# A Fourier mixing kernel on one core: its trips through DRAM cut into parts, its first transforms reordered, its stores given to another engine

## The chip, the cores and the metric

One core of one Trainium2 chip. The metric is device time in microseconds (us). Times quoted are medians of the fast runs of a kernel. A ratio is the mean time of one kernel's fast runs over the mean time of the fast runs of the kernel before that ran in the same rounds on the same chip, so it is not quite the quotient of the two medians. A difference under 2% counts as the same.

A *product* is one matrix instruction of TensorE. A transfer *lands* when its data are in place and what waits for it may go on. The *partitions* of a tile are its rows (up to 128 here); the *free dimension* runs along a row. A transform ends where the profile models the end of its last product.

## The reference, cut to what matters

```python
def _attn_ref(x, w_r, w_i, b_r, b_i):              # x: (8, 3072, 256)
    X = np.fft.rfft(x, axis=1)
    Yr = Xr @ w_r - Xi @ w_i + b_r
    Yi = Xr @ w_i + Xi @ w_r + b_i
    # soft threshold by 0.01 on both parts
    return np.fft.irfft(Y, n=x.shape[1], axis=1)

def _moe_ref(x, mu_k, mu_r, w_k, w_v, w_r):
    x_prev = x shifted by one token
    xk = mu_k * x + (1.0 - mu_k) * x_prev;  xr = the same with mu_r
    k = np.maximum(xk @ w_k, 0.0)                  # 256 -> 1024
    return sigmoid(xr @ w_r) * (k * k @ w_v)       # 1024 -> 256
```

The 3072 points of a sequence are taken as 96 x 32. A batch (there are 8) passes through a *first* transform (96 points), a *middle* (32 points, channel mixing, threshold, 32 points back), a *last* transform (96 points back), and then the products of tokens.

## The kernel before: the parts that matter

Between first and middle, and again between middle and last, partition and free dimension change places. The kernel does that by storing a tile to DRAM and fetching it back in another order: the *bounce* of A (fetched as A2) and the bounce of V (fetched as V2). TensorE takes its products in the order in which the program issues them, and a small simulation at build time decides that order: each unit of work has a due time and needs, and the constants `READ_US` and `WRITE_US` are the simulation's estimates of a fetch and a store.

```python
def first(b, t0, t1):                  # bounce of A
    ...
    def store(k):
        nc.sync.dma_start(out=Adr[b][:, 8 * q:8 * q + 8, :], in_=a)
        ...
        if q == 3:
            at(k + WRITE_US, fetch)
    def fetch(k):                      # 4 copies, each into 32 partitions
        A2[b] = a2_pool.tile([128, NG, D], BF16, name="A2")
        for cj in range(4):
            nc.sync.dma_start(out=A2[b][32 * cj:32 * cj + 32],
                              in_=Adr[b][24 * cj:24 * cj + 24].rearrange("g n d -> n g d"))
        done["A2", b] = k + READ_US
    ...
    needs = [("x", b, q), "FT"] + [("mid", 0)] * (b == 1)

def middle(b, t0, t1):                 # bounce of V
    ...
    def fetch(k):                      # 4 copies, each into 96 partitions
        for q in range(4):
            V2[b, q] = v2_pool.tile([96, 8, D], BF16, name="V2")
        for q in (2, 3, 0, 1):
            nc.sync.dma_start(out=V2[b, q], in_=Vdr[b][:, 8 * q:8 * q + 8, :])
        done["V2", b] = k + READ_US

def v_unit(t, p):                      # the end of a tile of tokens
    ...
    for xx in range(4):
        nc.sync.dma_start(out=rows[hh, half, xx], in_=o[32 * xx:32 * xx + 32])
```

## Time and profile before

| | before |
|---|---|
| median, fast runs | 670.4 us as given; 669.4 in the rounds with the changed kernel |
| span of the profiled run | 662.8 us |
| batch 0: middle starts, last transform ends | 32.0, 84.3 us |
| TensorE's last product ends | 656.8 us |

TensorE is the bound: it is busy for 593.6 of 662.8 us. The two fetches: 384 KB go into 32 partitions of A2, or into 96 of V2, in six to seven us from issue to landing. The profile gives the size of a copy and not the partitions it goes to; those stand in the program.

### The profile page before, as it was taken

The page shows a single profiled execution, that of the slowest core. Times are in us where ns is not written, and L with a number is a line of the kernel's source. Part 1 is how long each engine was busy: PE and PEld are TensorE (multiplying, and loading weights), DVE is VectorE, ACT ScalarE, POOL GpSimd, SP SyncE. Part 2 cuts the span into 40 slices and gives each one's busy share as a digit, 9 for nine tenths or more (in the row PEclk, how much of TensorE's full clock was granted, in tenths as well). Part 3 has the DMA queues.
Part 4 walks back from the last instruction along what each step waited for, and adds up shares of the span by engine and source line. Part 5 has one row for each costly group of instructions (what it writes and reads, how often), then busy time and mean ns, then how long its engine had stood idle before and what let it go on. Part 6 is the DMA issues. An engine that isn't in the chain of part 4 may idle for free.

```text
span 662.8 us, 12033 instructions
## 1 busy us (share of the span) xinstructions
PE 593.6 (90%) x4722; PEld 435.5 (66%) x4801; DVE 483.8 (73%) x732; ACT 443.5 (67%) x469; POOL 25.2 (4%) x57
## 2 busy tenths in 40 slices
PE   4295379999999989998999989999999999999996
PEld 1273247777776767765777767766777777777764
DVE  5164368788778877797678787688677896788883
ACT  6254357767777767776577767778687767766662
POOL 5021000000000000000000000000000000000000
PEclk9689579999999999999999999999999999999999
DMA  8697996362247954488155874379233852362223
GB/s 182 119 189 166 290 213 121 79 183 65 57 112 175 230 128 111 103 227 197 33 128 128 237 146 96 88 202 207 86 104 104 223 113 68 78 183 56 65 72 88
DMA packets 75593, 90.33 MB, mean 136 GB/s; under 512 B 8976, under 2 KB 59920, under 8 KB 75536
## 3 DMA queue, kind: packets, MB, share of 16 engines
q1 hardware_dynamic: 69696, 75.53, 44.5%
q0 software_dynamic: 5840, 14.03, 12.5%
q8 instruction: 37, 0.61, 0.4%
q14 instruction: 20, 0.16, 0.1%
HBM read 53.22 MB, written 50.33 MB: 156 GB/s over the span
## 4 chain that ended last, share of the span: by engine, by line
PE 66%; DMA 17%; ACT 6%; DVE 5%; issue 3%; SPq 1%; POOL 0%; DVEq 0%; ACTq 0%; POOLq 0%
PE banks L617 22%; PE banks L575 19%; PE banks L394 11%; DMA Adr<-A 7%; DMA A<-Adr 6%; PE banks L600 4%; ACT rl L581 3%; PE banks L361 3%; PE banks L418 2%; PE banks L383 2%; ACT A L234 2%; PE banks L287 2%; DMA Vdr<-V 1%; DVE V L236 1%; PE banks L489 1%
## 5 line engine op out<-in xcount | busy, mean ns | idle before, releaser
L581 ACT ACTIVATE rl<-banks 128x1024 bf16<-128x1024 f32 x192 | 195.0, 1029 | 86.1 <-PE banks L575 73.2
L575 PE MATMUL banks<-xk,wk 128*128 128x512 bf16 x706 | 191.1, 383 | 4.0 <-DVE xk L553 1.4
L617 PE MATMUL banks<-wv,k 128*128 128x256 bf16 x1536 | 184.5, 274 | 0.4 <-DVE k L587 0.3
L587 DVE TENSOR_TENSOR k<-rl 128x1024 bf16<-128x1024 bf16 x192 | 131.8, 687 | 53.6 <-ACT rl L581 53.5
L617 PEld LDWEIGHTS <-k 128*128 128x128 bf16 x1536 | 150.3, 98 | 30.1 <-issue 1.8
L575 PEld LDWEIGHTS <-wk 128*128 128x128 bf16 x768 | 73.4, 98 | 57.9 <-issue 4.3
L394 PEld LDWEIGHTS <-XT 128*128 128x128 bf16 x768 | 75.4, 98 | 23.9 <-issue 0.8
L402 ACT ACTIVATE r<-banks,neglam 128x1024 bf16<-128x1024 f32 x48 | 53.4, 1113 | 40.6 <-PE banks L394 39.4
L406 DVE SCALAR_TENSOR_TENSOR Y<-banks,r 128x1024 bf16<-128x1024 f32 x48 | 58.5, 1222 | 28.1 <-ACT r L402 28.0
L394 PE MATMUL banks<-wr,XT 128*128 128x256 bf16 x384 | 73.8, 274 | 0.9
L394 PE MATMUL banks<-wi,XT 128*128 128x256 bf16 x384 | 73.8, 274 | 0.0
L553 DVE SCALAR_TENSOR_TENSOR xk<-diff,muk,YT 128x512 bf16<-128x512 bf16 x96 | 70.0, 746 | 0.6
L553 DVE SCALAR_TENSOR_TENSOR xr<-diff,mur,YT 128x512 bf16<-128x512 bf16 x96 | 69.2, 745 | 0.0
L624 DVE TENSOR_TENSOR o<-banks,rg 128x1024 f32<-128x1024 f32 x48 | 58.5, 1218 | 7.7 <-PE banks L617 7.7
L234 ACT ACTIVATE XT<-banks 128x1024 bf16<-128x1024 f32 (+2 forms) x39 | 37.8, 970 | 35.4 <-PE banks L361 23.5
L234 ACT ACTIVATE A<-banks 96x1024 bf16<-96x1024 f32 x49 | 49.2, 1020 | 17.6 <-DMA Adr<-A 12.0
L287 PE MATMUL banks<-xs,FT 96*96 96x512 bf16 x128 | 39.5, 420 | 19.0 <-ACT A L234 11.7
L600 PE MATMUL banks<-wrm,xr 128*128 128x256 bf16 x384 | 49.8, 272 | 3.5 <-ACT rl L581 2.2
L234 ACT ACTIVATE YT<-banks 128x768 bf16<-128x768 f32 x51 | 39.9, 815 | 16.2 <-PE banks L489 16.2
L605 ACT ACTIVATE rg<-banks 128x1024 bf16<-128x1024 f32 x48 | 49.2, 1026 | 1.9 <-PE banks L600 1.9
L600 PEld LDWEIGHTS <-xr 128*128 128x128 bf16 x384 | 37.1, 97 | 14.1 <-issue 3.8
L234 ACT ACTIVATE V<-banks 128x1024 bf16<-128x1024 f32 x33 | 33.8, 1023 | 9.9 <-PE banks L418 8.1
(91 smaller groups left out, 401.8 us busy)
## 6 DMA issues: line engine op xcount, KB each, us to landing
out_dram<-o SPq DMA_DIRECT2D x192, 128.0 KB, 2.2
xs<-in_x_dram POOLq DMA_DIRECT2D x32, 384.0 KB, 8.1
Adr<-A SPq DMA_DIRECT2D x32, 384.0 KB, 6.6
A<-Adr SPq DMA_DIRECT2D x32, 384.0 KB, 6.6
Vdr<-V SPq DMA_DIRECT2D x192, 64.0 KB, 1.8
V<-Vdr SPq DMA_DIRECT2D x32, 384.0 KB, 6.2
wk<-in_moe_w_k_dram POOLq DMA_DIRECT2D x1, 512.0 KB, 5.4
wv<-in_moe_w_v_dram POOLq DMA_DIRECT2D x1, 512.0 KB, 8.4
```

The costliest lines, as they stand in the source:

```text
L234: nc.scalar.activation(out, in_, AF.Copy, bias=0.0, scale=1.0)
L287: nc.tensor.matmul(ps[:96, 512 * i:512 * i + 512], FT, xt[:, 4 * p + 2 * i:4 * p + 2 * i + 2, :], start=True, stop=True)
L394: nc.tensor.matmul(o, lhs, w[:, c, :], start=False, stop=(w is wi and c == NCD - 1 and (i == 1 or not (u or half))))
L402: nc.scalar.activation(r1, ps, AF.Relu, bias=neglam, scale=1.0)
L406: nc.vector.scalar_tensor_tensor(out=y, in0=ps, scalar=LAM, in1=r1, op0=ALU.add, op1=ALU.min)
L553: nc.vector.scalar_tensor_tensor(out=m[:, c, :], in0=df[:, c, :], scalar=mu[:, c:c + 1], in1=yp[:, c, :], op0=ALU.mult, op1=ALU.add)
L575: nc.tensor.matmul(ps[:, 512 * f:512 * f + 512], wk[:, c, 128 * ff:128 * ff + 128], xk[:, c, :], start=(c == 0), stop=(c == NCD - 1))
L581: nc.scalar.activation(rl, ps, AF.Relu, bias=0.0, scale=1.0)
L587: nc.vector.tensor_tensor(out=k2, in0=rl, in1=rl, op=ALU.mult)
L600: nc.tensor.matmul(ps[:, 256 * q:256 * q + 256], xr[:, c, 128 * q:128 * q + 128], wrm[:, c, :], start=(c == 0), stop=(c == NCD - 1))
L617: nc.tensor.matmul(ps[:, 256 * q:256 * q + 256], K2[t][:, ff, 128 * q:128 * q + 128], wv[:, ff, :], start=(ff == 0), stop=(ff == NCF - 1))
L624: nc.vector.tensor_tensor(out=o.rearrange("p q d -> p (q d)"), in0=ps, in1=rg, op=ALU.mult)
```

## The change

Its intent: shorten the start by letting batch 0's bounces travel in parts while work goes on, take batch 1's first transform out of batch 0's way, keep TensorE's clock up with products that nobody reads, and free SyncE's queue of the output's stores.

Cut to its core, a few lines shortened to words:

```diff
-    v2_pool: 4 buffers of [96, 8, D]          # cut: one pool line
+    v2_pool: 1 buffer of [96, N2, D]
@@ bounce of A: after each quarter's store (batch 0), after each second one (others)
-                    if q == 3:
-                        at(k + WRITE_US, fetch)
+                    if b == 0:
+                        at(land, lambda k: fetch(k, q, 1))
+                    elif q % 2:
+                        at(land, lambda k: fetch(k, q - 1, 2))
...
-                        nc.sync.dma_start(out=A2[b][32 * cj:32 * cj + 32],
-                                          in_=Adr[b][24 * cj:24 * cj + 24].rearrange("g n d -> n g d"))
+                        sl = slice(8 * q0, 8 * (q0 + nq))
+                        nc.sync.dma_start(out=A2[b][32 * cj + 8 * q0:32 * cj + 8 * (q0 + nq)],
+                                          in_=Adr[b][24 * cj:24 * cj + 24, sl].rearrange("g n d -> n g d"))
...
-            needs = [("x", b, q), "FT"] + [("mid", 0)] * (b == 1)
+            needs = [("x", b, q), "FT"] + [("last", 0)] * (b == 1)
@@ bounce of V: stored as it lies, fetched by 16 groups after tile 3 and 8 after tile 5
-                        nc.sync.dma_start(out=V2[b, q], in_=Vdr[b][:, 8 * q:8 * q + 8, :])
+                        r0 = 24 * cj + g0
+                        nc.sync.dma_start(
+                            out=V2[b][r0:r0 + ng],
+                            in_=Vdr[b][32 * cj:32 * cj + 32, g0:g0 + ng].rearrange("n g d -> g n d"))
...
-                if u == NU - 1 and b >= 1:
+                if u == 0 and b >= 1:
                     needs.append(("last", b - 1))
@@ output stores
-                    nc.sync.dma_start(out=rows[hh, half, xx], in_=o[32 * xx:32 * xx + 32])
+                    nc.gpsimd.dma_start(out=rows[hh, half, xx], in_=o[32 * xx:32 * xx + 32])
@@ unread products, twice twelve, 16 rows each (called "spin" in the program)
+    tab += [Unit(19.0, 2.6, [("A2p", 0, 1)], spin(lambda: A2[0][0:16, 0, 0:128], lambda: A2[0][0:16, 1:3, :])),
+            Unit(44.0, 2.6, [("V2p", 0, 0), ("mid", 0)],
+                 spin(lambda: V2[0][0:16, 0, 0:128], lambda: V2[0][0:16, 1:3, :]))]
@@ estimates and due times (more due times cut)
-    READ_US, WRITE_US = 7.0, 5.0
+    READ_US, WRITE_US = 6.0, 5.0
-    START = 60.0
+    START = 50.0
```

More of the change, by code (lines that the diff above doesn't have):

```diff
@@ L57 @@
     a_pool, a2_pool, xt_pool, xt0_pool = pool("ap", 3), pool("a2p", 2), pool("xtp", 3), pool("xt0p", 1)
-    r1_pool, ym_pool, v_pool, v2_pool = pool("r1p", 2), pool("ymp", 3), pool("vp", 3), pool("v2p", 4)
+    r1_pool, ym_pool, v_pool, v2_pool = pool("r1p", 2), pool("ymp", 3), pool("vp", 3), pool("v2p", 1)
     yt_pool, mx_pool, rl_pool, k2_pool = pool("ytp", 2), pool("mxp", 2), pool("rlp", 3), pool("k2p", 2)
@@ L211 @@
     heap, seq = [], itertools.count()
-    free = {"pe": 0.0, "act": 8.0, "dve": 14.0}
+    free = {"pe": 0.0, "act": 6.0, "dve": 13.3}
     done, slots = {}, {}
@@ L298, in store @@
                     nc.sync.dma_start(out=Adr[b][:, 8 * q:8 * q + 8, :], in_=a)
-                    done["a", b, q] = k + WRITE_US
+                    land = k + (3.0 if b == 0 else WRITE_US)
+                    done["a", b, q] = land
                     n = 4 * b + q + 4
@@ L303, in store, with fetch @@
                         done["x", n // 4, n % 4] = k + 9.0
-                    if q == 3:
-                        at(k + WRITE_US, fetch)
-                def fetch(k):
-                    A2[b] = a2_pool.tile([128, NG, D], BF16, name="A2")
-                    for cj in range(4):
-                        nc.sync.dma_start(out=A2[b][32 * cj:32 * cj + 32],
-                                          in_=Adr[b][24 * cj:24 * cj + 24].rearrange("g n d -> n g d"))
-                    done["A2", b] = k + READ_US
-                    if b == 0:
-                        nc.gpsimd.tensor_copy(out=junk, in_=A2[0][:, 0, 0:1])
-                        load_big()
-                        for n in range(4):
-                            load_x(1, n)
-                            done["x", 1, n] = k + 18.0
+                    if b == 0:
+                        at(land, lambda k: fetch(k, q, 1))
+                    elif q % 2:
+                        at(land, lambda k: fetch(k, q - 1, 2))
+                def fetch(k, q0, nq):
+                    if q0 == 0:
+                        A2[b] = a2_pool.tile([128, NG, D], BF16, name="A2")
+                    for cj in range(4):
+                        sl = slice(8 * q0, 8 * (q0 + nq))
+                        nc.sync.dma_start(out=A2[b][32 * cj + 8 * q0:32 * cj + 8 * (q0 + nq)],
+                                          in_=Adr[b][24 * cj:24 * cj + 24, sl].rearrange("g n d -> n g d"))
+                    done["A2p", b, q0] = k + (3.0 if b == 0 else READ_US)
+                    if q0 + nq == 4:
+                        done["A2", b] = done["A2p", b, q0]
+                        if b == 0:
+                            nc.gpsimd.tensor_copy(out=junk, in_=A2[0][:, 0, 0:1])
+                            load_big()
+                            for n in range(4):
+                                load_x(1, n)
+                                done["x", 1, n] = k + 20.0
                 at(end, evac)
-            needs = [("x", b, q), "FT"] + [("mid", 0)] * (b == 1)
-            if q == 3 and p == 1 and b >= 2:
+            needs = [("x", b, q), "FT"] + [("last", 0)] * (b == 1)
+            if q == 0 and p == 0 and b >= 2:
                 needs.append(("mid", b - 2))
@@ L420, in issue @@
                 if u == 0:
-                    Vdr[b] = dram.tile([2 * 48, N2, D], BF16, name="Vdr")
+                    Vdr[b] = dram.tile([128, NG, D], BF16, name="Vdr")
                 vt = v_pool.tile([128, 4, D], BF16, name="V")
@@ L429, in store, with fetch @@
                 def store(k):
+                    nc.sync.dma_start(out=Vdr[b][:, 4 * u:4 * u + 4, :], in_=vt)
+                    land = k + (3.0 if b == 0 else WRITE_US)
+                    done["v", b, u] = land
+                    if u == 3:
+                        at(land, lambda k: fetch(k, 0, 16))
+                    elif u == NU - 1:
+                        at(land, lambda k: fetch(k, 16, 8))
+                def fetch(k, g0, ng):
+                    if g0 == 0:
+                        V2[b] = v2_pool.tile([96, N2, D], BF16, name="V2")
                     for cj in range(4):
+                        r0 = 24 * cj + g0
                         nc.sync.dma_start(
-                            out=Vdr[b][24 * cj + 4 * u:24 * cj + 4 * u + 4].rearrange("g n d -> n g d"),
-                            in_=vt[32 * cj:32 * cj + 32])
-                    done["v", b, u] = k + WRITE_US
-                    if u == NU - 1:
-                        at(k + WRITE_US, fetch)
-                def fetch(k):
-                    for q in range(4):
-                        V2[b, q] = v2_pool.tile([96, 8, D], BF16, name="V2")
-                    for q in (2, 3, 0, 1):
-                        nc.sync.dma_start(out=V2[b, q], in_=Vdr[b][:, 8 * q:8 * q + 8, :])
-                    done["V2", b] = k + READ_US
+                            out=V2[b][r0:r0 + ng],
+                            in_=Vdr[b][32 * cj:32 * cj + 32, g0:g0 + ng].rearrange("n g d -> g n d"))
+                    done["V2p", b, g0] = k + (3.0 if b == 0 else READ_US)
+                    if g0 + ng == NG:
+                        done["V2", b] = done["V2p", b, g0]
                 if u == NU - 1:
@@ L488, in issue @@
                     for c in range(NCD):
-                        nc.tensor.matmul(pv[:, c, :, i, :], V2[b, n2 // 8][:, n2 % 8, 128 * c:128 * c + 128],
+                        nc.tensor.matmul(pv[:, c, :, i, :], V2[b][:, n2, 128 * c:128 * c + 128],
                                          FI, start=True, stop=True)
@@ L669, in table_gi, with spin, issue @@
         return issue
+    def spin(lhs, rhs):
+        def issue(ps, h, end):
+            for _ in range(12):
+                nc.tensor.matmul(ps[:, 0:512], lhs(), rhs(), start=True, stop=True)
+            release(h, end + 0.2)
+        return issue
     def tables(k):
@@ L680 @@
         s = START + P * (b - 1)
-        fb += first(b, 0.0, 1.0) if b == 0 else first(b, *((45.0, 52.0) if b == 1 else (s - 0.9 * P, s - 0.1 * P)))
-        fa += middle(b, 20.0, 44.0) if b == 0 else middle(b, s, s + 0.5 * P)
-        fc += last(b, 55.0, 60.0) if b == 0 else last(b, s + 0.75 * P, s + 0.95 * P)
+        if b == 0:
+            fb += first(b, 0.0, 1.0)
+            fa += middle(b, 20.0, 44.0)
+            fc += last(b, 45.0, 50.0)
+        else:
+            fb += first(b, START, START + 1.0) if b == 1 else first(b, s - 0.9 * P, s - 0.2 * P)
+            fa += middle(b, s + (0.2 * P if b == 1 else 0.0), s + 0.5 * P)
+            fc += last(b, s + 0.75 * P, s + 0.95 * P)
     for t in range(NT):
@@ L700 @@
     for q in range(4):
-        done["x", 0, q] = 5.0 + 3.3 * q
-    done["FT"] = 8.0
-    at(13.3, tables)
+        done["x", 0, q] = 6.0 + 2.8 * q
+    done["FT"] = 5.0
+    at(16.0, tables)
     tab = [Unit(18.0, 0.1, ["FT"], table_fi)]
     tab += [Unit(18.0 + n, 0.5, ["G"], table_gi(n)) for n in range(3)]
+    tab += [Unit(19.0, 2.6, [("A2p", 0, 1)], spin(lambda: A2[0][0:16, 0, 0:128], lambda: A2[0][0:16, 1:3, :])),
+            Unit(44.0, 2.6, [("V2p", 0, 0), ("mid", 0)],
+                 spin(lambda: V2[0][0:16, 0, 0:128], lambda: V2[0][0:16, 1:3, :]))]
     streams = [tok, val, fa, fb, fc, tab]
-    at(60.0 - 7.0, lambda k: mix_tokens(0, k))
+    at(START - 7.0, lambda k: mix_tokens(0, k))
     place, held, t = [0] * len(streams), {}, 0.0
```

## The prediction

> **What bounds the kernel now.** I read the page's busy shares and slices first, then a table of the engines by stretch, then the first 100 us of the chain that ended last, TensorE's waits, and SyncE's waits.
>
> The table by stretch (stretch, its length, busy us of PE, weight loads, DVE, ACT, POOL, then granted clock, DMA share, GB/s):
>
> ```profile
> PEclk9689579999999999999999999999999999999999
> 0.00:32.00 32.00, 10.38 (x42) 5.50 (x43) 11.33 (x49) 14.07 (x15) 8.41 (x26) 0.86 0.78 156
> 32.00:57.00 25.00, 21.87 (x182) 17.39 (x186) 14.46 (x18) 13.30 (x14) 5.19 (x9) 0.91 0.89 169
> 57.00:76.00 19.00, 6.03 (x22) 2.54 (x20) 6.99 (x6) 6.28 (x7) 3.03 (x6) 0.68 0.99 238
> 76.00:86.00 10.00, 7.56 (x72) 6.06 (x73) 4.05 (x11) 5.45 (x8) 0.39 (x1) 0.57 1.02 259
> 86.00:98.00 12.00, 7.19 (x30) 3.56 (x30) 7.15 (x12) 5.11 (x7) 0.62 (x2) 0.72 1.08 237
> 98.00:657.00 559.00, 540.61 (x4380) 400.46 (x4453) 438.71 (x641) 399.26 (x422) 7.59 (x15) 1.00 0.52 126
> ```
>
> From 98 us on TensorE is busy 97% at full clock: there it is the bound, and only its own waits can be saved. Before 98 us it is busy 53 of 98 us, partly at half clock, with the DMA near 1.0 from 57 us. The chain says which transfers hold it (start, length, what):
>
> ```profile
> 18.48 2.98 DMA Adr<-A
> 23.06 8.78 DMA A<-Adr
> 42.39 6.81 DMA Vdr<-V
> 49.27 2.98 DMA Vdr<-V
> 60.30 11.49 DMA Adr<-A
> 73.20 8.43 DMA Adr<-A
> 83.54 8.54 DMA A<-Adr
> ```
>
> These are bounces through DRAM: batch 0's first transform out and back (18 to 32 us), its middle's result out (42 to 52), then batch 1's first transform (60 to 92). The last is in the way of batch 0: TensorE's queue is in order, and batch 1's first products stand ahead of batch 0's last transform in it. TensorE's waits (total, times, longest):
>
> ```profile
> PE banks L344 <- DMA A<-Adr: 23.5, 5, 12.4
> PE banks L287 <- ACT A L234: 11.7, 1, 11.7
> PE banks L287 <- DMA xs<-in_x_dram: 7.0, 2, 6.0
> PE banks L489 <- DMA V<-Vdr: 3.6, 4, 1.6
> ```
>
> The 23.5 us are 12.4 (batch 0), 3.4 (batch 1), and in the later timeline 2.36 at 236 us, 2.79 at 312 and 2.59 at 390. A further 1.62 at 465 is put down to ACT, at the same product. The 11.7 us is the jam at 61 to 73 us: the copies that free PSUM wait for a tile whose store has not landed. And SyncE, whose one queue issues every bounce and every output store:
>
> ```profile
> SPq L633 <- DVE o L624: 134.8, 25, 10.2
> SPq L310 <- DMA Adr<-A: 55.2, 11, 10.4
> ```
>
> A queue that waits 135 us for the output's last multiplication holds the bounces behind it.
>
> [...]the array goes to half clock[...]. The trace agrees: 0.57 and 0.68 after idle stretches; a 512-wide product then takes 0.43 us instead of 0.216. [...]GpSimd's input loads take 0.51 us to issue in busy stretches[...].
>
> **The change part by part.** (a) Batch 0's first bounce in quarters. Now the four stores leave at 8.96 to 18.48 us, the return starts at 21.56 and lands at 31.84. Afterwards three quarters travel while the last is made. Its copy goes to VectorE, where it no longer waits for the sine tables on ACT (13.8 to 16.7 us), only for a GpSimd iota that ends at 15.82: bsel to 16.3, copy of 1.22 to 17.6. Store of 2.98: 20.7. Four issues of about 0.45 and 96 KB each on 8 engines: a 512 B packet has a median of 35 ns in the records, so 96 packets per engine are 3.4 us, plus about 1: 26 us, against 31.8.
>
> (b) Twelve unread products before the middle. They wait for the second quarter (about 20 us) and the table products (end about 20.7), take 12 x 0.43 = 5.1 us, and end at 25.8, just as the data lands. They add nothing, and the middle starts near full clock: now it is cold until about 34.7, worth 1.3 us.
>
> (c) The middle takes 24.4 us (32.0 to 56.4). SyncE issues 24 small stores for it one after another (17.8 us of issuing), and ACT and DVE wait 1.6 and 2.4 us for a V tile to be stored. With 6 stores of 256 KB that goes, worth some 0.8 us at the end (the last two Y tiles). Middle: 22.2 us, end at 48.2.
>
> (d) V returns in 16 + 8 groups, the first during the middle. For the second: copy 1.0, store 2.9, issues and landing about 6 (512 KB on 8 engines, 128 packets x 30 to 40 ns = 3.8 to 5.1 us, plus 1): 58 us. The second twelve products fill part of that. The last transform, 64 products at 0.083 (52 took 4.34), ends at 64 us. Now it ends at 84.28. Gain 20.3 us.
>
> (e) Batch 1's first transform comes after. 24 of its 32 products (24 x 0.216 = 5.2 us) were already done by 84.28. That is work put off: loss 5.2 us.
>
> (f) The stretch after. Now, from 84.3 to 98.7 us, work worth 6.3 us at full clock (8 + 16 products of 0.216, 14 of 0.066, 2 of 0.11) takes 14.4: 8.1 lost. Afterwards about 19 us of TensorE work stands before batch 1's middle. ACT has for it, counted in the new order from the last transform on, 5 x 0.8 + 9 x 1.03 + 10 x 1.03 + 2 x 1.03 + 1.28 = 27 us, and DVE 26 us, both from about 58. So they set the pace to about 85: 4.5 us lost. Batch 1's return, behind a store at about 75 and beside batch 2's input loads, lands at 84 to 88: 2.5 more. Gain 8.1 - 7 = 1 us.
>
> (g) Later batches come back in halves, off a queue without output stores. Between the last first-stage product and the middle stand 20 us of TensorE work in both orders. Now the way round took 22.5 (216 to 236.1: store 8.5, return 8.8). With half as much in the second return it is 15 to 18. The waits 2.36 + 2.79 + 2.59 + 1.62 = 9.4 us go, and 1 us of half clock after 312. I keep 1.4: gain 9. Against it: the second part of V, on 8 engines, has 12.7 us of work to hide behind instead of 15.7, and needs 11 to 13: 0.5 us in each of six batches, loss 3.
>
> (h) The end: GpSimd issues the last four stores at some 0.5 us each, as SyncE does at 0.43, with a somewhat longer landing: loss 1 us.
>
> Sum: 20.3 - 5.2 + 1 + 9 - 3 - 1 = 21.1 us, and 670.4 - 21.1 = 649.
>
> **The rivals.** First, the gain at the start is taken back by ACT and DVE. For it: without middle products a tile of tokens costs TensorE 8.0 us (16 x 0.216 + 8 x 0.13 + 32 x 0.109), DVE 7.6 (4 x 0.69 + 0.69 + 4 x 0.745 + 1.22), so DVE is almost the bound. Against it: their backlog is finite, and the later middles have slack. If the stretch loses 12 us instead of 7: 654. Second, narrow transfers make V's second part the new wait: 2 us in each of six batches instead of 0.5, and two more at the start: 660. [...]against it, a V return of 1.5 MB now lands 9 us after its issue in traffic (210.7 to 219.7), and the new one carries 0.5 MB. Third, GpSimd as issuer is late or blocks the input loads behind an output that is not ready. Against it: inputs are loaded about a batch ahead, and 192 issues x 0.5 us are 96 us in 590. It would show as products waiting for xs, and cost 5 to 10 us. Fourth, better than reckoned: quarters land by 24 us and A2 never waits again: 641.
>
> **Range and chances.** The start is the largest term and the surest in direction: order alone takes batch 1's jam away from batch 0. I give it 4 us either way, the stretch after it 4, waits in later batches 5; added as squares, some 8. Range 640 to 660. Two per cent is 657.0; only two rivals at once reach it: faster 0.86, within 2% 0.13, slower 0.01.
>
> **What would show it.** Batch 0's A2 landed at 25 to 27 us, its last transform ended at 62 to 66, clock 1.0 when the middle starts. Batch 1's middle starts at 84 to 89 us with ACT and DVE over 90% busy before it. Waits for A2 in later batches under 2 us in sum; waits for V about 3. SyncE's wait for o gone, GpSimd's in its place. Wrong would be: A2 of batch 0 at 30 us or later, the last transform after 70, products waiting for xs, or V waits over 8 us.

Two of its figures need the trace beside them. The 8 engines of (a), (d) and (g) had no run behind them when they were written. The changed kernel has its 16 engines busy 0.54 of the time while batch 0's last quarters travel (34 to 47 us) and 0.49 around V's second part (83 to 93 us), about what 8 of 16 would give; its records do not say which engines those are. And in (b), the middle of the kernel before runs at half speed until 36.6 us, not 34.7: two products of 256 columns take 0.42 us from start to start at 34.06 us, and 0.22 at 36.86.

## More of the kernel before

From the page of the kernel before: the busy times (us, share of the span, count), and two of the DMA issues (count, KB of one, us from issue to landing).

```profile
PE 593.6 (90%) x4722; PEld 435.5 (66%) x4801; DVE 483.8 (73%) x732; ACT 443.5 (67%) x469; POOL 25.2 (4%) x57
...
A<-Adr SPq DMA_DIRECT2D x32, 384.0 KB, 6.6
...
V<-Vdr SPq DMA_DIRECT2D x32, 384.0 KB, 6.2
```

## The result, and the profile after

803.6 us (802.4 to 808.1, four fast runs) against 669.4: ratio 1.202, 95% interval 1.196 to 1.207. The kernel became a fifth slower, far outside the range of 640 to 660.

Busy times and granted clock in the 40 slices, page of the changed kernel:

```profile
PE 615.8 (77%) x4746; PEld 445.5 (55%) x4825; DVE 491.5 (61%) x739; ACT 436.0 (54%) x462; POOL 118.8 (15%) x249
...
PEclk9668596996999799996999799996999789988997
```

TensorE's work has grown little, and DVE's and ACT's hardly at all. Of the 140 us more of span, TensorE stands still for 118 and is busy for 22: the 24 unread products (10.6 us), and work while the clock is low. Before, the clock was full from the seventh slice on; now it falls again in every batch. TensorE's waits say for what (us in total, times, longest):

```profile
PE banks L501 <- DMA V<-Vdr: 70.0, 5, 16.7
PE banks L501 <- issue: 24.3, 2, 15.6
PE banks L501 <- DMA Adr<-A: 14.9, 1, 14.9
PE banks L351 <- DMA A<-Adr: 14.9, 1, 14.9
PE banks L351 <- DMA Adr<-A: 12.8, 1, 12.8
```

L501 is the last transform's product, L351 the middle's first one. All three L501 lines stand at the same place, the first product of a batch that reads V2; together they are 109.2 us in eight waits, some 14 each, where the kernel before had 3.6 us in all. The names "issue" and "Adr<-A" for three of them are the profile's guess at which semaphore came last. The two L351 waits are for A2.

By stretch (length, busy us of PE, weight loads, DVE, ACT, POOL, then clock, DMA share, GB/s), the changed kernel:

```profile
0.00:26.00 26.00, 10.58 (x41) 5.36 (x41) 11.37 (x49) 14.41 (x15) 8.43 (x25) 0.98 0.80 145
26.00:50.00 24.00, 8.07 (x33) 4.03 (x34) 0.59 (x1) 1.41 (x2) 2.56 (x5) 0.50 0.53 52
50.00:64.00 14.00, 13.63 (x121) 10.81 (x122) 8.99 (x13) 7.69 (x8) 2.56 (x6) 0.92 1.16 211
64.00:90.00 26.00, 10.41 (x53) 5.39 (x51) 4.91 (x5) 4.61 (x5) 0.00 (x0) 0.67 0.80 124
90.00:125.00 35.00, 25.78 (x174) 16.76 (x176) 23.98 (x37) 24.91 (x27) 4.50 (x9) 0.84 0.75 139
125.00:789.00 664.00, 547.16 (x4329) 403.15 (x4403) 440.40 (x635) 383.00 (x406) 98.78 (x202) 0.92 0.60 111
```

The row to look at is 26 to 50 us: little computes, and the DMA moves 52 GB/s, a third of what it does before the stretch, though its engines are busy half the time (0.53, for 0.80 before). The transfers take long for the bytes they carry. The chain of the changed kernel has them (start, length, what):

```profile
21.03 12.05 DMA Adr<-A
...
34.23 12.76 DMA A<-Adr
...
72.14 10.29 DMA Vdr<-V
...
83.63 9.62 DMA V<-Vdr
```

The last quarter's store takes 12.1 us to land where the same store took 2.98, probably because it shares the way with fetches of the quarters before it (in spread_tail below, where those fetches go to partitions that lie apart, it takes 4.3). The last quarter then takes 12.8 us from the issue of its fourth copy, more than the whole A2 took from the same point before (8.78), for a quarter of the bytes. A2 is complete at 47.2 us, not at 26. And three lines of TensorE's timeline, changed kernel (start, length, what, count, and the idle time before it):

```profile
27.05 5.30 PE L687 MATMUL banks<-A 16*128 16x512 bf16 x12 [5.45 <-DMA A<-Adr]
47.23 0.59 PE L351 MATMUL banks<-G,A 128*128 128x256 f16 x2 [14.87 <-DMA A<-Adr]
47.60 1.70 PE L368 MATMUL banks<-G,A 128*128 128x128 f16 x14
```

The twelve unread products are there, and the middle behind them still began at half clock: its 128-wide products start 0.107 us apart, which is half speed (0.94 us for fourteen at full speed, in combined2 below).

What a transfer moves while only it is under way shows in the DMA view of a stretch. Changed kernel, 34 to 47 us (copies of 96 KB into 8 neighbouring partitions):

```profile
DMA packets 1248, 0.61 MB, mean 47 GB/s; under 512 B 55, under 2 KB 1248, under 8 KB 1248
```

Kernel before, 24.6 to 31.8 us (copies of 384 KB into 32 partitions):

```profile
DMA packets 2221, 1.11 MB, mean 154 GB/s; under 512 B 50, under 2 KB 2221, under 8 KB 2221
```

Same packets of 512 bytes, a third of the rate. Batch 0's sixteen quarter copies carry 1.57 MB; at 47 GB/s that is 33 us, and they ran from 14.8 to 47.2 us.

### The profile page after: what moved, and what is told of

It is laid out like the page before. It is cut to its first block, busy times and chain, and to the rows that moved or that the text cites. A ratio compares the mean times of both kernels' runs of the same rounds, so it can differ in the third digit from the quotient of the medians.

```text
span 802.7 us, 11991 instructions
## 1 busy us (share of the span) xinstructions
PE 615.8 (77%) x4746; PEld 445.5 (55%) x4825; DVE 491.5 (61%) x739; ACT 436.0 (54%) x462; POOL 118.8 (15%) x249
## 4 chain that ended last, share of the span: by engine, by line
PE 54%; DMA 28%; ACT 6%; DVE 4%; issue 3%; SPq 2%; POOL 0%; POOLq 0%; ACTq 0%; DVEq 0%
PE banks L629 17%; PE banks L587 13%; DMA Vdr<-V 11%; PE banks L401 10%; DMA V<-Vdr 8%; DMA Adr<-A 6%; PE banks L612 3%; PE banks L501 3%; ACT rl L593 2%; PE banks L368 2%; PE banks L425 2%; DMA xs<-in_x_dram 2%; PE banks L390 2%; DMA A<-Adr 2%; SPq L450 1%
## 5 line engine op out<-in xcount | busy, mean ns | idle before, releaser
L629 PE MATMUL banks<-wv,k 128*128 128x256 bf16 x1536 | 193.1, 281 | 2.4 <-ACT rg L617 1.7
L645 POOL DMA_DIRECT2D out_dram<-o x192 | 93.5, 494 | 581.5 <-DVE o L636 518.8
L629 PEld LDWEIGHTS <-k 128*128 128x128 bf16 x1536 | 154.6, 101 | 37.5 <-issue 3.9
L501 PE MATMUL banks<-FI,V 96*128 96x96 f16 x512 | 34.6, 224 | 110.2 <-DMA V<-Vdr 70.0
L501 PEld LDWEIGHTS <-V 96*128 96x128 bf16 x512 | 30.7, 108 | 119.9 <-issue 73.1
L515 DVE COPY YT<-YT 128x576 bf16<-128x576 bf16 x16 | 4.9, 309 | 87.8 <-ACT YT L234 87.8
```

The lines of the kernel that those rows point to most:

```text
L501: nc.tensor.matmul(pv[:, c, :, i, :], V2[b][:, n2, 128 * c:128 * c + 128], FI, start=True, stop=True)
L629: nc.tensor.matmul(ps[:, 256 * q:256 * q + 256], K2[t][:, ff, 128 * q:128 * q + 128], wv[:, ff, :], start=(ff == 0), stop=(ff == NCF - 1))
L645: nc.gpsimd.dma_start(out=rows[hh, half, xx], in_=o[32 * xx:32 * xx + 32])
```

## Theory and rivals

The two DMA views above compare copies with the same packets that differ, among other things, in the partitions they go to: 384 KB into 32 moved 154 GB/s, 96 KB into 8 neighbouring ones 47. An estimate from these two: if the rate goes with the number of neighbouring partitions, 8 for 32 move a quarter of 154, 39 GB/s. A copy of a quarter of the rows would then take about as long as the copy of all of them, and four quarters would cost about four times the whole. Why the partitions should matter no trace here shows; whether they do, a run can.

- **Theory P (partitions):** neighbouring partitions make the parts slow.
- **Rival E (engines):** copies into 8 partitions are slow because they use only 8 of the 16 DMA engines, as the prediction had them.
- **Rival D (DRAM):** the narrow parts read a narrower window of DRAM.
- **Rival G (GpSimd):** output stores from GpSimd are in the way.
- **Rival O (order):** the new order of TensorE's queue is what loses.

## The experiments

**bench: the fetches alone.** Its output is wrong, which doesn't matter for the time. Four copies as the kernel makes them, then one small DVE copy that waits for them, each case twice.

```diff
+    for cj in range(4):
+        dst = T[32 * cj:32 * cj + (parts - 1) * dstep + 1:dstep]     # dstep: partition step
+        s = Adr[24 * cj:24 * cj + 24, 0:(parts - 1) * sstep + 1:sstep]
+        nc.sync.dma_start(out=dst, in_=s.rearrange("g n d -> n g d"))
+    nc.vector.tensor_copy(out=tag, in_=T[:, :, 0])                   # waits for the four
```

> Fetches alone, four copies each, timed from the first issue to the copy that waits for all of them; wrong result on purpose. In the changed kernel a fetch into 16 partitions (0.75 MB) and one into 8 (0.38 MB) both took some 10 to 11 us, where the 32-partition one of before (1.5 MB) takes 8.8. Theory 1, SBUF side: [...]Then spreading the same partitions (every 4th, every 2nd) makes them fast: 8 spread about 4 us, 16 spread about 5.5 us, and a wider source leaves them at 9 to 11. Theory 2, DRAM side: the engines read neighbouring 512 B pieces out of a window of 4 or 8 KB. Then a wider source (every 4th, every 2nd row) makes them fast and spreading the partitions leaves them at 9 to 11. Theory 3, the number of engines or one partition per engine: neither helps.

Second pass, DVE's timeline; the time in brackets is DVE's wait for the four copies (w: 32 partitions, h: 16, q: 8; "spread": every second, fourth or third partition; "wide": DRAM rows further apart; v: V's two parts, 16 and then 8 groups):

```profile
113.41 0.18 DVE L64 COPY w<-T 128x24 bf16<-128x24 bf16 x1 [7.03 <-DMA T<-Adr]
123.10 0.18 DVE L64 COPY h<-T 128x24 bf16<-128x24 bf16 x1 [9.51 <-DMA T<-Adr]
132.43 0.18 DVE L64 COPY q<-T 128x24 bf16<-128x24 bf16 x1 [9.14 <-DMA T<-Adr]
138.53 0.18 DVE L64 COPY h16spread<-T 128x24 bf16<-128x24 bf16 x1 [5.92 <-DMA T<-Adr]
143.66 0.18 DVE L64 COPY q8spread<-T 128x24 bf16<-128x24 bf16 x1 [4.94 <-DMA T<-Adr]
154.43 0.18 DVE L64 COPY h16wide<-T 128x24 bf16<-128x24 bf16 x1 [10.59 <-DMA T<-Adr]
164.89 0.18 DVE L64 COPY q8wide<-T 128x24 bf16<-128x24 bf16 x1 [10.27 <-DMA T<-Adr]
175.02 0.19 DVE L73 COPY v<-W 96x32 bf16<-96x32 bf16 x1 [9.95 <-DMA W<-Vdr]
185.74 0.19 DVE L73 COPY v<-W 96x32 bf16<-96x32 bf16 x1 [10.53 <-DMA W<-Vdr]
192.49 0.19 DVE L73 COPY v8spread<-W 96x32 bf16<-96x32 bf16 x1 [6.55 <-DMA W<-Vdr]
```

Three lines mislead: the copies of w and of the first v write another tile than the case ahead of them, and were issued while it still ran. So the waits of w and v are cut short, and q8wide ran beside the first copies of v. From its first issue, at 102.14 us, w took 11.3 us, and 12.0 in the first pass, where nothing ran ahead of it. A quarter of the bytes (q, 9.1 us; 10.0 in the first pass) takes four fifths of that. Eight partitions again, but four apart, take 4.9. Engine count cannot be it: q and q8spread have the same dimensions. (The share that E speaks of is there: in the first pass the 16 engines are busy 0.46 of the time around q, 37.9 to 47.5 us, and 1.00 around h, 28 to 37.5 us; and h, with its engines busy, took 10.7 us to q's 10.0.) Nor DRAM: h16wide, which ran alone, took 10.6 us to h's 9.5. P stands, E and D fall. V's second part, 0.5 MB, takes 10.5 us, and 6.6 on every third partition.

**spstore: the changed kernel with its output stores on SyncE.** Rival G.

```diff
-                    nc.gpsimd.dma_start(out=rows[hh, half, xx], in_=o[32 * xx:32 * xx + 32])
+                    nc.sync.dma_start(out=rows[hh, half, xx], in_=o[32 * xx:32 * xx + 32])
```

> The changed kernel with the output stores issued by SyncE again. Theory of the narrow fetches: still 790 to 815 us, since the waits for V and A2 stay. Rival, GpSimd as the issuer slows the bounces: back to 650 to 690 us.

810.2 us, ratio 1.212 (1.205 to 1.219). G falls as the cause of the loss.

**vold: V's bounce as before** (parts, buffers, its order, and the second twelve unread products out), all else as changed.

```diff
-    V2[b] in parts of 16 and 8 groups, one buffer, u == 0 waits for the batch before
+    V2[b, q] in four copies of 96 partitions, four buffers, u == NU - 1 waits
```

> The changed kernel with the second bounce (V) as before, its second set of unread products left out; the first bounce stays in pieces. Theory of the narrow fetches: the 110 us of idle before the last transforms go, the waits for A2 stay (47 us at the start and some later): 680 to 710 us. Rival, GpSimd stores or the new order at fault: 760 us or more.

728.5 us, ratio 1.091 (1.085 to 1.098). V's part of the change costs 75 us; I had expected more, so A2's share was under-estimated.

**bothwhole: both bounces whole, no unread products**; the order of the first transforms and the stores on GpSimd remain.

```diff
-                    if b == 0:
-                        at(land, lambda k: fetch(k, q, 1))
-                    elif q % 2:
-                        at(land, lambda k: fetch(k, q - 1, 2))
+                    if q == 3:
+                        at(land, lambda k: fetch(k, 0, 4))
```

> The changed kernel with both bounces whole as before and no unread products: what is left is the later first transform of batch 1, the new order of the first transforms and GpSimd's output stores. Theory of the narrow fetches: at most the time of before, 645 to 670 us. Rival, order or GpSimd at fault: 720 us or more.

673.6 us, ratio 1.009 (1.006 to 1.012). So A2's parts cost another 55 us, the two bounces together 130 of the 134 us lost, and what is left of the change is itself slower than the kernel before by 0.9%. I had given it a chance to be faster; O is a small loss, not the loss.

**spread: bothwhole with A2 in quarters in every batch, laid over every fourth partition**, the tables permuted to match.

```diff
-                        nc.sync.dma_start(out=A2[b][32 * cj + 8 * q0:32 * cj + 8 * (q0 + nq)],
+                        nc.sync.dma_start(out=A2[b][32 * cj + q0:32 * cj + q0 + 29:4],
+    # partition 4 i + q of each block of 32 holds row n2 = 8 q + i
```

> As bothwhole (673.6 us), but the first bounce comes back in quarters again, in every batch, with the rows of a quarter laid over every 4th partition[...] instead of 8 neighbours[...]; the tables of batch-independent angles follow the new order, so the result stays right. [...]batch 0's middle starts at 24 to 27 us instead of 31.2, batch 1's wait of 4.8 us and the later waits for A2 (4.9 us together) go: 655 to 668 us. If small pieces are slow for another reason (number of copies, 8 engines): as slow as vold, 700 us or more.

671.1 us, ratio 1.002 (0.995 to 1.008). This is the direct test in the kernel: no fewer parts than vold has (there quarters in batch 0 and halves in the others), other partitions, and the loss of 55 us is gone. (vold's twelve unread products are out as well; in its trace they end at 32.6 us, and A2 lands at 46.9.) The expected gain at the start did not come: A2 was there at 31.7 us, not 24 to 27 (its profiled run was a slow one, but the next run's, fast, has 31.1). A copy with a partition step took SyncE 0.66 us to issue (chain of spread_tail), where one into 8 neighbours took mostly 0.34 (chain of the changed kernel); sixteen are 10.6 us, and stores of later quarters stand behind them. Batch 0's first store, beside the input loads, takes 5.86 us to land (chain of the changed kernel) where I had reckoned with 2.98.

**spread_tail: the same, with the last six tiles' stores on SyncE.** In the changed kernel, before_pool and bothwhole, whose last stores are GpSimd's, the span ends 13.6 us after TensorE's last product; where they are SyncE's, 6.0 (the kernel before, both_tail) to 6.4 (combined2). In the trace's records a drain of GpSimd of 9.87 us starts at 792.06 in the changed kernel, and the span ends 0.8 us after it; in the kernel before, whose GpSimd has nothing to do late, one of 11.40 us lies at 442 us.

```diff
-                    nc.gpsimd.dma_start(...)
+                    (nc.sync if t >= NT - 6 else nc.gpsimd).dma_start(...)
```

> spread, with the output stores of the last six of 48 tiles issued by SyncE again. In the kernels whose last stores GpSimd issues the span ends 13.5 us after TensorE, and in the others 6.0; the trace has a GpSimd drain of 9.9 us there. If it is the drain of recent GpSimd transfers, this run is 6 to 8 us faster than spread; if it is something else about the program (a fixed cost of many GpSimd transfers), no change.

663.5 us, ratio 0.992 (0.986 to 0.998): 7.5 us better, as expected, and 0.8% faster than the kernel before.

**bothwhole_sp: bothwhole with all stores on SyncE**, so that of the change only the order of the first transforms is left, with the estimates and due times that make it.

```diff
-                    nc.gpsimd.dma_start(out=rows[hh, half, xx], in_=o[32 * xx:32 * xx + 32])
+                    nc.sync.dma_start(out=rows[hh, half, xx], in_=o[32 * xx:32 * xx + 32])
```

> bothwhole with all output stores issued by SyncE: what is left of the change is the order of the first transforms alone. If GpSimd's stores cost only the end (7.5 us) and gain little: 664 to 669 us. If they relieve SyncE's queue by more than that: 674 us or more, with waits for A2 and V back.

673.6 us, ratio 1.006 (1.000 to 1.012), between the two expectations. The trace shows a gain given back: batch 0's last transform ends at 73.4 us (before: 84.3), but batch 1's middle starts at 104.5 (before: 92.1), since its first transform now begins only behind that last transform.

**before_pool: the kernel before with GpSimd's stores and nothing else.**

```diff
-                    nc.sync.dma_start(out=rows[hh, half, xx], in_=o[32 * xx:32 * xx + 32])
+                    nc.gpsimd.dma_start(out=rows[hh, half, xx], in_=o[32 * xx:32 * xx + 32])
```

> The kernel before with nothing changed but the output stores issued by GpSimd. End 7.5 us longer, waits for A2 in later batches (9.4 us) partly gone: 666 to 675 us. If GpSimd as issuer holds up the bounces or the inputs: over 680.

680.3 us, ratio 1.018 (1.011 to 1.024), worse than expected. The tail (13.6 us for 6.0) explains 7.6 of some 12 us. TensorE's waits for V grew from 3.6 to 14.1 us in its trace; why they did was not settled.

**bench_clock: which products count for the clock.** Products alone, 512 wide, after idle stretches. Its output is wrong, which doesn't matter for the time.

```diff
+    phase("rows16", [(16, 128, 48), (128, 128, 40)], 2)      # (rows, columns, count)
+    phase("rows128", [(128, 128, 40), (16, 128, 60), (128, 128, 30)], 8)
+    phase("rows64", ...); phase("rows32", ...); phase("cols16", [(128, 16, 48), ...], 8)
```

> Products alone, all 512 columns wide, after idle stretches of TensorE (result wrong on purpose). Five sets: 48 products that use 16 of the 128 rows and then 40 that use all 128; 40 full, 60 with 16 rows, 30 full; 48 with 64 rows then 40 full; 48 with 32 rows then 40 full; 48 with 16 of 128 columns then 40 full. If step (b) failed because products with 16 rows don't count as work for the clock: the 48 products of 16 rows run at 0.43 us each to their end (about 20 us), and the full ones behind them reach 0.216 only after a further 4 to 5 us; in the second set the clock falls back to half during the 60 products of 16 rows (13 us at 0.216 if it lasts). If it failed for another reason (twelve products, 5.3 us, were too few, or the gap behind them undid it): the 16-row products reach 0.216 after 4 to 5 us just as full ones do.

Stretches of it; busy time over count is the spacing (from the top: 16 rows from idle; all rows behind them; 16 rows behind full ones; 64 rows; 32 rows; 16 columns):

```profile
24.00:40.00 16.00, 16.00 (x39) 5.26 (x38) 12.45 (x3) 0.00 (x0) 1.00 1.01 418
47.00:52.00 5.00, 5.00 (x24) 2.21 (x23) 3.50 (x1) 0.00 (x0) 1.00 1.02 419
...
113.00:123.00 10.00, 10.00 (x24) 3.38 (x23) 8.23 (x2) 0.00 (x0) 0.50 0.00 0
...
164.00:180.00 16.00, 16.00 (x39) 5.41 (x38) 12.45 (x3) 0.00 (x0) 0.50 0.00 0
...
234.00:250.00 16.00, 16.00 (x39) 5.25 (x37) 12.45 (x3) 0.00 (x0) 0.50 0.00 1
...
306.00:312.00 6.00, 6.00 (x30) 2.48 (x29) 0.00 (x0) 0.00 (x0) 1.00 0.00 0
```

Products with 16, 32 or 64 rows stayed at half speed for 20 us on end, 0.43 us from start to start; full ones reached 0.216 within 3 to 6 us, and products of 16 columns did too. (The quotients of the table, 0.41 and 0.21, come out low because products cut by the edges of a stretch are counted.) In the second set the clock fell to half about 4 us into the 16-row products though TensorE was never idle. (The clock column says 1.00 in the first stretch, where the spacing says half: believe the spacing.) So the change's unread products could not bring the clock up: four times as many did not.

**both_tail: bothwhole, last six tiles' stores on SyncE.**

```diff
-                    nc.gpsimd.dma_start(...)
+                    (nc.sync if t >= NT - 6 else nc.gpsimd).dma_start(...)
```

> Both bounces whole again, no unread products, GpSimd as issuer of the output stores, except those of the last six tiles, which SyncE issues. The theory of the tail (GpSimd's drain of about 10 us at the end) says 666 us: 673.6 less the 7.6 us by which the tail is longer with GpSimd's stores, and a tail of 6.0 us. If the gain of the run with the spread quarters came from the quarters instead: 672 to 674.

666.9 us, ratio 0.999 (0.996 to 1.003): the tail theory's 666. Against bothwhole_sp, which differs only in who issues the stores of the first 42 tiles, TensorE waits 11.8 us for V instead of 18.7: some relief for SyncE's queue is there, once the tail is gone. spread_tail's further 0.7% lies within the two intervals.

**early12: both_tail with batch 1's first twelve first-stage products ahead of batch 0's last transform**, the last four behind it, and batch 2's loads held back until batch 1's A2 has landed.

```diff
-            needs = [("x", b, q), "FT"] + [("last", 0)] * (b == 1)
+            needs = [("x", b, q), "FT"] + [("last", 0) if q == 3 else ("mid", 0)] * (b == 1)
```

> As the run before it, and batch 1's first 12 first-stage products stand ahead of batch 0's last transform, the last 4 behind it, so that part of batch 1's round trip is under way while batch 0's last transform waits; batch 2's inputs are held back until batch 1's return has landed. Theory that the order alone only shifts a wait (gain at batch 0's last transform, loss at batch 1's middle): with the split the last transform of batch 0 still ends at 73 to 76 us and batch 1's middle starts at 92 to 96 us instead of 101 to 108, so 658 to 662. Rival (the bounds after 98 us take it all back): 664 to 668.

664.3 us, ratio 0.995 (0.991 to 0.999). Batch 0's last transform ends at 74.9 us and batch 1's middle starts at 90.9, both as wanted; 9.6 us won against both_tail at that middle (100.5) are 2.6 at the end, so most of it is taken back behind, as the rival had it.

**combined: spread_tail and early12 together, and 26 unread products of all 128 rows** (identity by table) before batch 0's middle.

```diff
+    tab += [Unit(19.0, 8.0, ["G", "GI"], spin(lambda: ident, lambda: G.rearrange("p g a b c -> p (g a b c)")[:, 0:512]))]
```

> Everything that helped, together: quarters laid over every fourth partition in every batch, V whole, the last six tiles' stores on SyncE, batch 1's first 12 first-stage products ahead of batch 0's last transform, and 26 unread products that use all 128 rows (identity by table) between the table products and batch 0's middle. If products of all rows count for the clock, the middle of batch 0 starts at full clock and is 2.5 us shorter than the 31.1 to 66.5 us (start of middle to start of last transform) of the run before, minus whatever the unread products delay it. With the gains of the two runs (0.992 and 0.995 of the kernel before) at least partly adding: 656 to 661 us, ratio 0.985 to 0.99. Rival (the bounds after 98 us take it back): 662 to 665, and a clock that is full at 32 us all the same.

661.8 us, ratio 0.990 (0.987 to 0.993). The unread products stood in the wrong place: the needs that I gave them put them behind the middle's first sixteen products (they ran from 33.26 to 40.44 us), and the rest of the middle stood behind them.

**vnarrow and vspread: what in V costs.** One run had undone V's parts, its single buffer and its order at once. These two keep buffer, order and the times of the parts, and A2 whole. vspread lays V's groups on every third partition and permutes the table to match.

```diff
-                            out=V2[b][r0:r0 + ng],                  # r0 = 24 * cj + g0, 16 or 8 neighbours
+                                out=V2[b][r0:r0 + 22:3],            # r0 = 24 * cj + c, 8 groups each
+        # partition 24 cj + 3 a + c holds group 8 c + a
```

> The changed kernel with batch 0's and the others' first bounce whole again and without the unread products; V's bounce in 16 and 8 neighbouring partitions with its one buffer and its order, as the change has them. If the costs of the two bounces add: 803.6 less the 55 us that the quarters and halves of A2 cost, so 745 to 752 us, with products waiting 70 us and more for V.

> The run before it with V's groups 8c to 8c+7 laid on every third partition (24 j + 3 a + c)[...]; 12 fetches of 128 KB in place of 4 of 256 and 4 of 128; parts, buffers and order are the same. If neighbouring partitions are what the V part costs: the second part lands about 4 us sooner and the first 4 us sooner in each batch, and the SyncE queue with its bounces of A2 is freed by as much: 690 to 715 us. If it is the single buffer of V, its order in TensorE's queue, or the pieces as such: 740 to 752 as the run before.

vnarrow 749.1 us (1.121, 1.117 to 1.125): 54.5 below the changed kernel, so the costs of the two bounces add. vspread 715.9 us (1.069, 1.066 to 1.072), just above the 690 to 715 expected: 33 of V's 75 us are the neighbouring partitions. In batch 0 the store behind the first part lands in 5.1 us for vnarrow's 10.5, and the second part 4.7 us after its last issue for 8.8. That is less than all of the 75. TensorE still waited for V (vspread):

```profile
PE banks L504 <- DMA V<-Vdr: 27.7, 3, 16.1
PE banks L504 <- issue: 20.0, 3, 8.9
```

**vspread_late: one estimate changed.** The simulation that orders TensorE's queue believes that a part of V is there 6 us after its store landed.

```diff
-                    done["V2p", b, g0] = k + (3.0 if b == 0 else READ_US)
+                    done["V2p", b, g0] = k + (3.0 if b == 0 else 2 * READ_US)
```

> The run before last on V (third-partition pieces, 715.9 us) with one number changed: the estimate that orders TensorE's queue takes 12 us instead of 6 from the store's landing until a part of V is there, so that more products of tokens stand ahead of each batch's last transform. If the 42 us that are left over against whole bounces come from an order made for a V that lands sooner than it does: 680 to 695 us and V waits of under 25 us in all. If they come from the single buffer and the serial order that it forces (a batch's first V product behind the transform of the batch before): 705 to 720.

689.4 us, ratio 1.029 (1.025 to 1.034). Another 26.5 us: they were an order built for a V that lands sooner than it does, with too little work placed ahead of the last transform. The 15.8 us left over bothwhole (the single buffer, its dependency, more issues on SyncE) were not separated; nor was the same estimate tried on bothwhole, which may gain by it too.

**combined2: combined with 34 unread products of all rows ahead of the middle.**

```diff
-    tab += [Unit(19.0, 8.0, ["G", "GI"], ...)]      # 26
+    tab += [Unit(20.5, 2.0, ["G"], ...)]            # 34
```

> The combined version with the 26 unread products (34 now) ahead of the middle of batch 0 in TensorE's queue; in the run before my estimate had placed them behind the middle's first products, where they delayed it by 7.2 us. If products of all rows count for the clock: those of the middle run at full clock from its first one (16 table products in 0.9 to 1.1 us instead of 2.1), and batch 0's last transform starts at 62 to 65 us instead of 72.3: ratio 0.983 to 0.988, 656 to 660 us. Rival (what is won before 98 us is taken back behind it): ratio 0.990 as the run before.

655.9 us, ratio 0.980 (0.977 to 0.982), all correct, and better than both kernels (at the 2% of a verdict, so that the verdict is unclear). TensorE's timeline, combined2:

```profile
21.46 8.69 PE L689 MATMUL banks<-G,ident 128*128 128x512 f16 x34
31.56 0.38 PE L357 MATMUL banks<-G,A 128*128 128x256 f16 x2 [1.41 <-DMA A<-Adr]
31.77 0.94 PE L374 MATMUL banks<-G,A 128*128 128x128 f16 x14
```

and early12, without them:

```profile
31.10 0.59 PE L350 MATMUL banks<-G,A 128*128 128x256 f16 x2 [9.49 <-DMA A<-Adr]
31.48 1.70 PE L367 MATMUL banks<-G,A 128*128 128x128 f16 x14
```

Fourteen products in 0.94 us for 1.70: the middle begins at full clock. The part of my expectation about batch 0 missed: its last transform starts at 69.0 us, not 62 to 65, because V's return is then what it waits for (9.0 us). Against combined, batch 1's middle starts 5.1 us sooner and the whole is 6 us shorter. How much of the 2% the unread products are worth by themselves was not measured: no run has everything but them.

## Why the prediction was wrong, point by point

| V parts | A2 parts | time, us |
|---|---|---|
| neighbours | neighbours | 803.6 (the change) |
| neighbours | whole | 749.1 (vnarrow) |
| whole | neighbours | 728.5 (vold) |
| every third partition | whole | 715.9 (vspread) |
| every third, order for a later V | whole | 689.4 (vspread_late) |
| whole | every fourth partition | 671.1 (spread) |
| whole | whole | 673.6 (bothwhole) |

- **(a), the step that failed first.** "96 packets per engine are 3.4 us, plus about 1": an estimate. A2 landed at 47.2 us, not 26. What was wrong in the term is the 35 ns. In the packet records of the traces (the pages show only sums of them) the 512-byte packets have a median of 36 ns over the whole kernel before, but 52 ns in the very fetch that was to be cut (24.6 to 31.8 us), and 88 ns in the quarters (changed kernel, 34 to 47 us): 96 of these and 1 us are 9.4 us, and bench's quarter took 9.1. In bench they are 86 ns in q and 27 in q8spread. The prediction asked how many engines a narrow copy uses; the question was which partitions it goes to, and bench shows 9.1 us against 4.9 at the same dimensions.
- **(b)** Products of 16 rows did not bring the clock up: in bench_clock 48 of them stayed at 0.43 us from start to start for 20 us. The products ran at 27.05 us as foreseen in kind, and the middle began at half clock. The idea was sound: with all rows it worked (combined2: fourteen products of the middle in 0.94 us for 1.70).
- **(c)** The middle, start to its last product, took 23.8 us for 22.2: right within its half-clock start. (The "17.8 us of issuing" were misread: that is the stretch from the first of the 24 stores to the last, and 10.7 us of it are issuing.)
- **(d)** The same term as (a): for V's second part 3.8 to 5.1 us, plus 1. Measured 9.6, behind a store that took 10.3 instead of 2.9. The last transform ended at 98.9 us instead of 64. Of these 34.9 us, 21.2 are A2, 1.6 the middle and 12.0 V.
- **(e), (f)** Not reached in the changed kernel, since the waits came first. In bothwhole_sp, where the order stands alone, the 10.9 us won at batch 0's last transform are 12.4 lost at batch 1's middle. The first rival, that the gain at the start is given back behind it, was right there, but through batch 1's round trip rather than through ACT and DVE.
- **(g), the most costly step.** "0.5 us in each of six batches" for V: measured some 14 us in each of eight, and the clock falls in each batch: its mean from 125 us on is 0.92, where the kernel before had 1.00 from 98 us on. Batch 0 accounts for 14.6 us of the loss at its last transform (98.9 for 84.3); from there to the end of TensorE's last product it is 690.3 us for 572.5, another 118. The prediction saw the condition ("12.7 us of work to hide behind ... needs 11 to 13") and rested a margin of nothing on a transfer time that it had not measured. It also overlooked that the work placed ahead of the wait is itself chosen by an estimate in the program (`READ_US`), so that a transfer slower than the estimate waits in full: 26.5 us by vspread_late.
- **(h)** GpSimd's stores at the end were given 1 us; the tail grew by 7.6. And the 135 us that SyncE waited for the output are waits and not issuing; taking them off its queue was worth about 7 us in the new order (673.6 for bothwhole_sp, 666.9 for both_tail, with intervals that overlap), and nothing that shows in the old one (before_pool).
- **The rivals.** The second, "narrow transfers make V's second part the new wait", named the right wait for a reason, the 8 engines, that was not the limit, and with one seventh of its size (2 us a batch for 14). The chances were drawn from spreads around the sum, 8 us, and left no room for one shared term being wrong by a factor of two to three; both bounces used that term. "Only two rivals at once" were to reach 657.0, but the second alone was put at 660.

The prediction's own list of what would show it wrong held: A2 of batch 0 at 30 us or later, the last transform after 70, V waits over 8 us.

## What to carry to other kernels

Cutting a transfer into groups of neighbouring partitions hardly shortened the parts here (in bench a quarter of the bytes took 9.1 us for the whole's 11.3). Cut along the free dimension, as V is cut in the kernel before (the products of batch 0 waited 0.8 to 1.6 us for each of its first three copies), or give each part partitions that lie apart. That took the loss away here, and no more: A2 landed no sooner in spread quarters than whole (31.1 us in spread_tail and in both_tail). When a wait is hidden by an order that is made at build time, put the measured landing into the order's estimates before judging a change. And before a term is used in every stage of a sum, measure it once by itself: one run of bare fetches would have settled this in advance.
